# Routing steps on VectorE moved to other groups of an attention and mixture-of-experts kernel

## Chip, cores and metric

The kernel runs on one core of one Trainium2 chip, as one launch. The metric is the device time of that core in microseconds (us). Engines are named as the profile names them: PE is TensorE, with PEld its weight loads; DVE is VectorE, ACT is ScalarE, POOL is GpSimd and SP is SyncE, which issues most of the DMAs. Every engine works through its own instructions strictly in the order in which they stand, so an instruction that waits holds everything behind it on that engine.

## What is computed

Attention over 4 batches, 8 heads, 768 positions and 64 columns, in which a query sees only the keys of its own cluster, and behind it a mixture of 8 experts, where each of the 3072 tokens with a positive skip score goes to one expert:

```python
q_assign = np.argmax(np.einsum('bhsd,hcd->bhsc', q_n, c_n), axis=-1)   # k_assign likewise
scores = np.where(q_assign[:, :, :, None] == k_assign[:, :, None, :], scale * q @ k.T, -1e9)
attn = softmax(scores); x = (attn @ v)                  # 3072 tokens x 512
do_compute = x @ w_skip > 0
e_idx = np.argmax(x @ w_gate, axis=1); gate_w = softmax(x @ w_gate)[e_idx]
out = x + do_compute * gate_w * (relu(x @ w1[e_idx]) @ w2[e_idx])
```

## The kernel before

**Attention.** The work is cut into 16 pairs of heads, numbered 0 to 15; four pairs make a batch, so batch 0 is pairs 0 to 3. A pair has 24 slots. A slot computes one 128x384 block of scores with two matmuls (L637, L638), its exponential on ACT (L640, tile PT) and one accumulation of exponentials on POOL (L646, L652, tile acc). In the same slot PE also makes one matmul for the next pair (L588), whose row maximum DVE takes (L590, tile M). Behind slots 1, 9 and 17 of each pair PE has no scores for a while: it multiplies the last eight exponential tiles with the values (16 matmuls of L663), turns maxima (L612), and at one of the three places sums, turns and scales an earlier pair's output (L703, L715, L766 on PE; the reciprocal L720 and the scaling L771 on DVE). These three places of a pair are called block A (behind slot 1), block B (behind slot 9) and block C (behind slot 17) below. In a block DVE has no maxima to take, and the other DVE work of the kernel stands there.

**PSUM banks.** All of this takes its PSUM banks from one queue (`take`, `give`): a bank goes out again some three and a half slots after it was last taken. A matmul whose bank is still to be read waits for the reader. In block B the banks of L715 and L766 come round at slots 12 and 13, so PE waits there if L720 or L771 is late.

**Routing.** When a batch's four pairs are done, its 768 tokens are routed: the expert and the gate weight of each (`route_gates`), then its place in the expert's list (`route_slots`). The steps of `route_slots` that matter here, all on DVE but one:

- rk, rank, hi, los (L971 to L982): the token's rank in its expert, small operations;
- oht (L986, two instructions of 128x384 each): the one-hots of the rank; hs (L990), cs and cum (L1016, L1018), small;
- rhs (L1000, two instructions): the right sides of the list matmuls; then six small matmuls on PE (L1005) and their addition into slotacc (L1009);
- cc, c1, ri, li, gi, lo, code (L1026 to L1040): small.

**What sets the order.** Every step has a time in slots, counted from the start of a pair; a heap writes the instructions of all engines out in the order of these times, and that order is the program (nothing reorders it later). The 20 entries of a row of `SLOTS` are the times of the steps above, counted from the start of the batch's last pair. So 73.7, 81.7, 89.7 are blocks A, B, C of the third pair after the batch's last, 97.7 is block A of the fourth, and so on. The first row of `SLOTS` is for batches 0 and 1 (last pairs 3 and 7, so their steps lie in pairs 6 to 8 and 10 to 12), the second for batch 2 (last pair 11, so pairs 14 and 15). Batch 3 is routed in another way at the end. Also in pair 14, `early_lists` (`PLAN["early"]`) makes a first list of tokens out of batch 2's sums: a matmul (L1190), eight small operations on DVE and a gather by POOL (L1218).

**Experts.** Behind the attention the experts run one after the other, bound by PE; no line of that stage is touched.

Of the kernel before, what the change touches and what calls it, by code (L numbers as in the profile page):

```python
# [49 lines left out]
    "hi": (-38.405, -38.40), "masks": (-32.5, 0.12), "lo": (-30.38, -22.38), "copies": (-22.1, -21.2, -21.1),  # L50
    "smax": (-21.6, 1.0, -0.2), "mneg": (-9.2, 4.0), "mrows": ((-6.5, 0.2, 0.05), (9.62, 0.1, 0.05)),
    "av": 1.6, "oT": (0.35, 3.55), "sums": 33.55, "recip": 33.64, "xout": (33.66, 49.55, 41.55),
    "route": (33.45, 41.5, 65.5), "early": (85.4, 100.9),
}

GATES = (41.62, 41.63, 41.64, 41.65, 41.66, 49.66, 49.67, 49.68, 49.69, 49.7, 49.71, 50.5,
         53.16, 53.17, 53.18, 65.67, 65.68, 65.69, 65.7, 73.66, 73.67)
SLOTS = ((73.69, 73.7, 73.71, 73.72, 81.67, 81.68, 81.69, 81.7, 81.71, 81.72, 89.66, 91.0, 91.2,
          97.66, 97.67, 97.68, 97.69, 97.7, 97.71, 97.72),
         (73.69, 73.7, 73.71, 73.72, 73.73, 73.74, 73.75, 73.76, 73.77, 81.66, 81.67, 84.4, 84.6,  # L60
          85.9, 85.91, 97.66, 97.67, 97.68, 97.69, 97.7))
FIRST = {
    0: {
        "load_v": -18.9, "sims": -20.0, "hi": (-19.9, -19.8, -19.7, -19.6), "assign": (-19.0, 0.1, 0.01, 0.01, 0.01, 0.01),
# [20 lines left out]
class Kernel:  # L85
# [780 lines left out]
    def route_slots(self, i, bt):  # L866

        wait = iter([(t,) for t in SLOTS[i == self.npair - HP - 1]])
        yield from self.route_c(i, bt * KT, KT, wait)
# [316 lines left out]
    def early_lists(self, i):  # L1186

        nc, const = self.nc, self.const
        cp = self.take("cp", [P, 1])
        nc.tensor.matmul(cp, lhsT=self.ones_bf, rhs=self.cum[:, :1], start=True, stop=True)  # L1190
        yield (85.67,)
        pad = self.rt.tile([P, 1], F32, name="pad")
        nc.vector.tensor_scalar(out=pad, in0=cp, scalar1=-1.0, scalar2=float(P), op0=ALU.mult, op1=ALU.add)
        self.give("cp")
        nc.vector.tensor_scalar(out=pad, in0=pad, scalar1=0.0, scalar2=self.ident[:, :1], op0=ALU.max, op1=ALU.mult)
        nc.vector.tensor_tensor(out=self.cum[:, :1], in0=self.cum[:, :1], in1=pad, op=ALU.add)
        acc = self.acc[:, :, 0, :1]
        rd, wr = self.slot_ids(acc, const, P, 1, "e")
        self.xe = const.tile([P, 1, DM], F32, name="xe")
        yield 0.2  # L1200
        self.gather(self.xe[:, 0, :], rd, self.ntok - S)
        yield (91.66,)
        self.early = wr, self.slot_gates(acc, const, P, 1, "e")
# [329 lines left out]
```

## Time and profile before

| | us |
|---|---|
| time, median of 3 runs | 641.73 (641.08 to 643.89) |
| profiled execution, device time | 641.93 |
| profiled execution, span from first to last instruction | 640.2 |
| PE busy | 619.7 (97%) |
| DVE busy | 504.1 (79%) |
| ACT busy | 409.3 (64%) |
| POOL busy | 361.9 (57%) |

Attention takes roughly the first 430 us of the span. Times in rows are us from the span's start. A row of the view in order of time gives start, duration, engine, line, operation, output<-inputs with their shapes, how many instructions it merges, and in brackets the idle time of the engine before it with what ended that. A released wait is put down to the event that came last. A matmul's duration is that of a pipelined instruction: what a matmul costs is read from one start to the next.

### The profile page before, as it was taken

The page shows a single profiled execution, that of the slowest core. Times are in us where ns is not written, and L with a number is a line of the kernel's source. Part 1 is how long each engine was busy: PE and PEld are TensorE (multiplying, and loading weights), DVE is VectorE, ACT ScalarE, POOL GpSimd, SP SyncE. Part 2 cuts the span into 40 slices and gives each one's busy share as a digit, 9 for nine tenths or more (in the row PEclk, how much of TensorE's full clock was granted, in tenths as well). Part 3 has the DMA queues.
Part 4 walks back from the last instruction along what each step waited for, and adds up shares of the span by engine and source line. Part 5 has one row for each costly group of instructions (what it writes and reads, how often), then busy time and mean ns, then how long its engine had stood idle before and what let it go on. Part 6 is the DMA issues. An engine that isn't in the chain of part 4 may idle for free.

```text
span 640.2 us, 12142 instructions
## 1 busy us (share of the span) xinstructions
PE 619.7 (97%) x3873; PEld 459.1 (72%) x3873; DVE 504.1 (79%) x1060; ACT 409.3 (64%) x885; POOL 361.9 (57%) x384
## 2 busy tenths in 40 slices
PE   7899999999999999999999989999999999999994
PEld 3567677676766776767767756646799899899793
DVE  6989888789998789899879996875889765855721
ACT  7378677787777786777877867833744644645510
POOL 7797787777788777867867886522133212121101
PEclk9999999999999999999999999999999999999998
DMA  7388759758775665565565542332395766765711
GB/s 215 90 220 195 210 158 237 215 166 217 219 210 154 175 184 149 153 173 171 147 171 162 133 116 63 125 91 106 110 315 193 248 244 201 247 195 180 244 40 36
DMA packets 54321, 110.09 MB, mean 172 GB/s; under 512 B 8599, under 2 KB 22807, under 8 KB 54256
## 3 DMA queue, kind: packets, MB, share of 16 engines
q1 hardware_dynamic: 51232, 101.92, 54.9%
q0 software_dynamic: 2624, 7.18, 3.4%
q8 instruction: 32, 0.52, 0.4%
q14 instruction: 33, 0.27, 0.1%
q10 hardware_dynamic: 400, 0.20, 0.1%
HBM read 60.93 MB, written 10.55 MB: 112 GB/s over the span
## 4 chain that ended last, share of the span: by engine, by line
PE 31%; DMA 10%; issue 9%; DVE 4%; ACT 0%; POOL 0%; POOLq 0%; DVEq 0%
DMA out<-yo,idw 7%; PE ps L663 6%; PE ps L637 4%; PE ps L638 3%; PE ps L588 3%; DMA xg<-out,idr 2%; PE ph L1066 2%; PE ph L1065 2%; PE ph L1067 2%; PE py L1066 1%; PE py L1065 1%; PE py L1067 1%; DVE M L590 1%; DMA PT<-out,idr 1%; PE ps L703 1%
## 5 line engine op out<-in xcount | busy, mean ns | idle before, releaser
L652 POOL TENSOR_TENSOR acc<-acc,PT 128x384 f32<-128x384 f32 x246 | 242.2, 1013 | 47.3 <-ACT PT L640 46.9
L590 DVE TENSOR_REDUCE M<-ps 128x1 f32<-128x384 f32 x384 | 199.6, 554 | 24.8 <-PE ps L588 24.5
L640 ACT ACTIVATE PT<-ps 128x384 f32<-128x384 f32 x384 | 179.7, 492 | 41.2 <-PE ps L638 30.2
L637 PE MATMUL ps<-D 102*128 102x384 f32 x384 | 135.9, 354 | 3.9 <-DVE M L590 2.7
L663 PE MATMUL ps<-PT,vt 128*64 128x385 f32 x768 | 135.6, 494 | 0.0
L588 PE MATMUL ps<-D 96*128 96x384 f32 x384 | 130.3, 346 | 2.2 <-ACT D L568 1.0
L638 PE MATMUL ps<-D 128*128 128x384 f32 x384 | 130.2, 339 | 0.0
L663 PEld LDWEIGHTS ps<-PT,vt 128*64 128x64 f32 x768 | 50.8, 136 | 69.0 <-issue 59.3
L637 PEld LDWEIGHTS ps<-D 102*128 102x128 f32 x384 | 72.8, 190 | 24.5 <-issue 6.6
L646 POOL TENSOR_TENSOR acc<-PT 128x384 f32<-128x384 f32 x64 | 55.6, 888 | 52.0 <-ACT PT L640 51.2
L1223 POOL DMA_INDIRECT out<-yo,idw x15 | 20.1, 1337 | 112.9 <-DVE yo L1099 102.6
L588 PEld LDWEIGHTS ps<-D 96*128 96x128 f32 x384 | 73.1, 191 | 6.3 <-ACT D L568 1.4
L638 PEld LDWEIGHTS ps<-D 128*128 128x128 f32 x384 | 73.1, 190 | 0.0
L1351 ACT ACTIVATE hh<-ph 128x256 fp32r<-128x256 f32 x56 | 21.5, 384 | 46.4 <-PE ph L1067 46.1
L1352 DVE SCALAR_TENSOR_TENSOR hl<-ph,hh 128x256 fp32r<-128x256 f32 x56 | 23.7, 423 | 33.6 <-ACT hh L1351 33.5
L1323 ACT ACTIVATE D<-wraw 128x1024 fp32r<-128x1024 f32 (+1 forms) x45 | 44.1, 1002 | 6.2 <-PE py L1067 4.7
L1065 PE MATMUL ph<-x2l,D 128*128 128x256 f32 x168 | 47.7, 284 | 0.0
L1066 PE MATMUL ph<-x2h,D 128*128 128x256 f32 x168 | 47.5, 283 | 0.0
L1065 PE MATMUL py<-D,hh 128*128 128x512 f32 x112 | 45.0, 402 | 0.0
L623 ACT ACTIVATE D<-ps,blocks 6x256 fp32r<-6x256 f32 x84 | 33.3, 457 | 12.7 <-PE ps L612 12.3
L1324 DVE TENSOR_TENSOR D<-wraw,D 128x1024 fp32r<-128x1024 f32 (+1 forms) x29 | 34.3, 1184 | 6.2 <-ACT D L1323 5.3
L1066 PE MATMUL py<-D,hh 128*128 128x512 f32 x84 | 33.0, 392 | 0.0
(312 smaller groups left out, 1030.7 us busy)
## 6 DMA issues: line engine op xcount, KB each, us to landing
wraw<-w SPq DMA_DIRECT2D x72, 512.0 KB, 4.7
D<-D SPq DMA_DIRECT2D x124, 192.0 KB, 3.4
raw<-qk SPq DMA_DIRECT2D x16, 768.0 KB, 6.1
D<-raw SPq DMA_DIRECT2D x60, 192.0 KB, 3.6
vt<-v SPq DMA_DIRECT2D x16, 384.0 KB, 4.2
out<-x SPq DMA_DIRECT2D x31, 192.0 KB, 2.9
D<-mk SPq DMA_DIRECT2D x120, 24.0 KB, 2.3
out<-yo,idw POOLq DMA_INDIRECT x15, 4.6
```

The costliest lines, as they stand in the source:

```text
L588: nc.tensor.matmul(sm, lhsT=c["qm"][a][0:96, j * P:(j + 1) * P], rhs=c["kb"][a][0:96, hf * HALF:(hf + 1) * HALF], start=True, stop=True)
L590: nc.vector.tensor_reduce(out=c["m"][:, j, a, hf:hf + 1], in_=sm, axis=AX.X, op=ALU.max)
L637: nc.tensor.matmul(ps, lhsT=c["kb"][a][:MR, ks], rhs=c["qm"][a][:MR, sl], start=True, stop=False)
L638: nc.tensor.matmul(ps, lhsT=c["kc"][a][:, ks], rhs=c["qc"][a][:, sl], start=False, stop=True)
L640: nc.scalar.activation(out=pt, in_=ps, func=AF.Exp, scale=D ** -0.5)
L646: nc.gpsimd.tensor_tensor(out=acc, in0=self.pt(i, s - 2)[:, :HALF], in1=pt, op=ALU.add)
L652: (nc.vector if dve else nc.gpsimd).tensor_tensor(out=acc, in0=acc, in1=pt, op=ALU.add)
L663: nc.tensor.matmul(av[a * D:(a + 1) * D, :], lhsT=c["vt"][:, kt, a * D:(a + 1) * D], rhs=self.pt(i, hf * 2 * KT + kt * 2 + a), start=(kt = ...
L1065: mm(ps, lhsT=ah, rhs=bl, start=first, stop=False)
L1066: mm(ps, lhsT=ah, rhs=bh, start=False, stop=False)
L1323: nc.scalar.activation(out=h[:, cs], in_=r[:, cs], func=AF.Copy)
L1324: nc.vector.tensor_tensor(out=l[:, cs], in0=r[:, cs], in1=h.bitcast(F32)[:, cs], op=ALU.subtract)
```

## The change

Only times in the tables change, and with them the order. No instruction is added, removed or altered; the orders of ACT and SP stay the same, and on POOL the gather of `early_lists` stands one accumulation later.

```diff
-    "route": (33.45, 41.5, 65.5), "early": (85.4, 100.9),
+    "route": (33.45, 41.5, 65.5), "early": (86.1, 100.9),
...
-SLOTS = ((73.69, 73.7, 73.71, 73.72, 81.67, 81.68, 81.69, 81.7, 81.71, 81.72, 89.66, 91.0, 91.2,
+SLOTS = ((73.69, 73.7, 73.71, 73.72, 81.67, 89.66, 89.67, 89.68, 89.69, 105.66, 105.67, 107.3, 107.5,
...
         cp = self.take("cp", [P, 1])
         nc.tensor.matmul(cp, lhsT=self.ones_bf, rhs=self.cum[:, :1], start=True, stop=True)
-        yield (85.67,)
+        yield (86.3,)
```

For batches 0 and 1 the second one-hot, hs, cs and cum go from block B to block C of pairs 6 and 10; both right sides go to block B of pairs 7 and 11 (they stood in blocks B and C of pairs 6 and 10), with their matmuls and the addition behind them; cc to li go from block A to block C of pairs 7 and 11, gi to code to block A of pairs 8 and 12. For batch 2 both one-hots, hs, cs and cum go from block A to block B of pair 14, ahead of the right sides, which stay there; its matmuls, the addition, cc, c1 and the steps of `early_lists` come 0.6 to 0.7 slots later.

DVE in pair 6 (batch 0), from block B on, before; rows is the last step of the next pair's cluster assignment, M the maxima, raw a subtraction for a later pair:

```order
L534 STREAM_TRANSPOSE rows<-oh 128x384
L986 TENSOR_TENSOR oht<-iota,los 128x384 x2
L990 TENSOR_TENSOR hs<-iota,hi 128x12
L1016 TENSOR_REDUCE cs<-ohd 128x8
L1018 TENSOR_TENSOR cum<-cum,cs 128x8
L1000 TENSOR_TENSOR rhs_2091<-rv,hs 128x30x8
L720 RECIPROCAL rs<-ps_87 128x3x2 x2
L771 TENSOR_TENSOR x<-ps_85,rs 128x384
```

The same place now:

```order
L534 STREAM_TRANSPOSE rows<-oh 128x384
L986 TENSOR_TENSOR oht<-iota,los 128x384
L720 RECIPROCAL rs<-ps_87 128x3x2 x2
L771 TENSOR_TENSOR x<-ps_85,rs 128x384
L590 TENSOR_REDUCE M_200<-ps_81 128x1
```

Only one one-hot is left between the assignment and the reciprocal; the other, hs, cs and cum stand in block C behind raw, where the second right side stood.

DVE in pair 14 (batch 2), block A to block B, as a piece of the difference:

```order
 L982 SCALAR_TENSOR_TENSOR los<-hi,rank 128x6
+L590 TENSOR_REDUCE M_200<-ps_84 128x1
+L590 TENSOR_REDUCE M_200<-ps_83 128x1
+L604 TENSOR_REDUCE MX_190<-M_199 128x3x2
+L590 TENSOR_REDUCE M_200<-ps_87 128x1
+L590 TENSOR_REDUCE M_200<-ps_85 128x1
+L590 TENSOR_REDUCE M_200<-ps_86 128x1
+L590 TENSOR_REDUCE M_200<-ps_88 128x1
+L590 TENSOR_REDUCE M_200<-ps_82 128x1
+L590 TENSOR_REDUCE M_200<-ps_85 128x1
 L986 TENSOR_TENSOR oht<-iota,los 128x384 x2
 L990 TENSOR_TENSOR hs<-iota,hi 128x12
```

The eight maxima of slots 2 to 9 now come ahead of the one-hots, and the one-hots stand where only the two right sides stood ahead of L720.

DVE in pair 7, block B, now (before, L534 was followed by L720 at once):

```order
L534 STREAM_TRANSPOSE rows<-oh 128x384
L1000 TENSOR_TENSOR rhs_2346<-rv,hs 128x30x8 x2
L720 RECIPROCAL rs<-ps_87 128x3x2 x2
L771 TENSOR_TENSOR x<-ps_85,rs 128x384
L590 TENSOR_REDUCE M_199<-ps_86 128x1
L590 TENSOR_REDUCE M_199<-ps_88 128x1
L1009 TENSOR_TENSOR slotacc<-slotacc,ps_84 128x80
```

Both right sides now stand ahead of the reciprocal of that block, and the addition into slotacc behind two maxima; pair 11 has the same.

## Rows read from the trace of the kernel before

**Rows 1.** In order of time, DVE, pair 6, block B.

```profile
181.38 1.87 DVE L986 TENSOR_TENSOR oht<-iota,los 128x384 bf16<-128x384 f32 x2
183.18 0.16 DVE L990 TENSOR_TENSOR hs<-iota,hi 128x12 bf16<-128x12 f32 x1
...
183.60 0.40 DVE L1000 TENSOR_TENSOR rhs<-rv,hs 128x240 bf16<-128x240 bf16 x1
183.92 0.26 DVE L720 RECIPROCAL rs<-ps 128x6 f32<-128x6 f32 x2
```

**Rows 2.** In order of time, DVE, pair 7, block B.

```profile
206.58 0.58 DVE L534 STREAM_TRANSPOSE rows<-oh 128x384 bf16<-128x384 bf16 x1
207.98 0.27 DVE L720 RECIPROCAL rs<-ps 128x6 f32<-128x6 f32 x2 [0.82 <-PE ps L715]
```

**Rows 3.** In order of time, PE, pair 6: L637 of slots 10 and 15.

```profile
182.31 0.42 PE L637 MATMUL ps<-D 102*128 102x384 f32 x1
...
186.09 0.34 PE L637 MATMUL ps<-D 102*128 102x384 f32 x1
```

**Rows 4.** The same two slots of pair 7.

```profile
208.02 0.42 PE L637 MATMUL ps<-D 102*128 102x384 f32 x1
...
210.72 0.34 PE L637 MATMUL ps<-D 102*128 102x384 f32 x1
```

**Rows 5.** Busy time by stretch: PE, PEld, DVE, ACT, POOL, granted clock, DMA share, GB/s.

```profile
381.50:385.00 3.50, 3.50 (x16) 1.24 (x16) 3.49 (x6) 1.88 (x4) 3.35 (x4) 0.51 0.00 0
...
183.00:186.00 3.00, 2.49 (x13) 1.92 (x12) 2.83 (x11) 1.87 (x5) 1.89 (x2) 1.00 0.59 146
```

**Rows 6.** In order of time, DVE, pair 14, block A.

```profile
375.83 1.70 DVE L986 TENSOR_TENSOR oht<-iota,los 128x384 bf16<-128x384 f32 x2
377.45 0.82 DVE L990 TENSOR_TENSOR hs<-iota,hi 128x12 bf16<-128x12 f32 x1
...
379.14 1.01 DVE L590 TENSOR_REDUCE M<-ps 128x1 f32<-128x384 f32 x2
```

**Rows 7.** In order of time, PE, pair 14: L637 of slots 5, 6, 9 and 10.

```profile
376.38 0.34 PE L637 MATMUL ps<-D 102*128 102x384 f32 x1
...
379.74 0.44 PE L637 MATMUL ps<-D 102*128 102x384 f32 x1 [2.67 <-DVE M L590]
...
381.45 0.43 PE L637 MATMUL ps<-D 102*128 102x384 f32 x1
...
387.88 0.42 PE L637 MATMUL ps<-D 102*128 102x384 f32 x1
```

**Rows 8.** In order of time, PE, pair 13: L637 of slots 9 and 10.

```profile
354.81 0.34 PE L637 MATMUL ps<-D 102*128 102x384 f32 x1
...
359.69 0.42 PE L637 MATMUL ps<-D 102*128 102x384 f32 x1
```

**Rows 9.** In order of time, DVE, pair 13, block B.

```profile
356.37 0.57 DVE L516 TENSOR_TENSOR eqc<-eqc,wts 128x384 f32<-128x384 f32 x1
...
359.64 0.27 DVE L720 RECIPROCAL rs<-ps 128x6 f32<-128x6 f32 x2 [0.81 <-PE ps L715]
```

**Rows 10.** In order of time, DVE, pair 14, block B.

```profile
383.03 2.08 DVE L1000 TENSOR_TENSOR rhs<-rv,hs 128x240 bf16<-128x240 bf16 x2
387.83 0.27 DVE L720 RECIPROCAL rs<-ps 128x6 f32<-128x6 f32 x2 [2.72 <-PE ps L715]
```

**Rows 11.** In order of time, POOL, pair 13, through block B.

```profile
353.86 6.04 POOL L652 TENSOR_TENSOR acc<-acc,PT 128x384 f32<-128x384 f32 x6
```

**Rows 12.** In order of time, POOL, pair 7, up to the end of block B.

```profile
204.80 3.42 POOL L652 TENSOR_TENSOR acc<-acc,PT 128x384 f32<-128x384 f32 x3
```

**Rows 13.** In order of time, PE, pair 6: list matmuls in slot 19, and what follows.

```profile
191.62 0.39 PE L1005 MATMUL ps<-rhs,oht 128*128 128x80 bf16 x6
191.84 0.42 PE L588 MATMUL ps<-D 96*128 96x384 f32 x1
```

**Rows 14.** In order of time, DVE, pair 6, behind block C's right side.

```profile
191.47 0.56 DVE L590 TENSOR_REDUCE M<-ps 128x1 f32<-128x384 f32 x1 [0.21 <-PE ps L588]
```

More of the change, by code (lines that the diff above doesn't have):

```diff
@@ L57 @@
          53.16, 53.17, 53.18, 65.67, 65.68, 65.69, 65.7, 73.66, 73.67)
-SLOTS = ((73.69, 73.7, 73.71, 73.72, 81.67, 81.68, 81.69, 81.7, 81.71, 81.72, 89.66, 91.0, 91.2,
-          97.66, 97.67, 97.68, 97.69, 97.7, 97.71, 97.72),
-         (73.69, 73.7, 73.71, 73.72, 73.73, 73.74, 73.75, 73.76, 73.77, 81.66, 81.67, 84.4, 84.6,
-          85.9, 85.91, 97.66, 97.67, 97.68, 97.69, 97.7))
+SLOTS = ((73.69, 73.7, 73.71, 73.72, 81.67, 89.66, 89.67, 89.68, 89.69, 105.66, 105.67, 107.3, 107.5,
+          113.66, 113.67, 113.68, 113.69, 121.66, 121.67, 121.68),
+         (73.69, 73.7, 73.71, 73.72, 81.66, 81.67, 81.68, 81.69, 81.7, 81.71, 81.72, 85.0, 85.2,
+          86.6, 86.61, 97.66, 97.67, 97.68, 97.69, 97.7))
 FIRST = {
```

## Prediction

> **What bounds the kernel now.** The first view to read is the page's busy times: PE is busy 97% of the span, so time can only be won where PE stands still or runs slowly. The second is the view in order of time for PE, read from the start of one score matmul (L637) to the next: an undisturbed slot takes 0.54 us, as slots 10 to 15 of pair 7 show (210.72 - 208.02 = 2.70 for five) [rows 4]. Measured in this way two kinds of place stand out among the slots that the change touches.
>
> The first is pair 6 behind block B. The same five slots take 186.09 - 182.31 = 3.78 us there [rows 3], 1.08 more than in pair 7, which has no routing step in that block. The view in order of time for DVE says why: the one-hots, hs, cs, cum and a right side stand ahead of the reciprocal L720, which begins 1.61 us behind slot 10's L637 (183.92 against 182.31) [rows 1, 3], while in pair 7 it begins 0.04 us ahead of it [rows 2, 4]. So it was 1.65 us late and cost PE 1.08: the first 0.57 us of lateness cost nothing, because the banks come round only later. Pair 10 repeats this (there are two such places).
>
> The second is pair 14. From slot 5 to slot 6 PE takes 379.74 - 376.38 = 3.36 us, 2.82 too many, and the wait is for a maximum on DVE [rows 7]. DVE came late because both one-hots, hs, cs and cum stood ahead of the maxima, from 375.83 to 379.14 [rows 6]. Behind that wait comes a second loss: from slot 9 to slot 10 PE takes 387.88 - 381.45 = 6.43 us [rows 7], in pair 13 only 359.69 - 354.81 = 4.88 [rows 8]. In this stretch the granted clock is 0.51, which is about the lower of the two levels, 1.2 GHz [rows 5]. PE had been idle for 2.67 us shortly before. DVE isn't the cause of this second loss: it had finished the right sides and waited 2.72 us for PE [rows 10]. I put these 1.55 us to the clock, and so to the wait.
>
> **Pairs 6 and 10.** One one-hot stays in block B, and hs, cs, cum, the second one-hot and the right side leave it. Two one-hots took 183.18 - 181.38 = 1.80 us [rows 1], so one takes about 0.9 or less. In pair 7 DVE was idle for 0.82 us ahead of L720 [rows 2], and with the 0.57 that cost nothing there are 1.39 us for it. The wait goes: 1.08 us twice, 2.16. In block C a one-hot (0.9) and the small steps (183.60 - 183.18 = 0.42) [rows 1] replace a right side (between 0.32 and the 1.04 of pair 14 [rows 10]); behind it DVE waited 0.21 for PE [rows 14]. The new work of 1.32 is 0.3 to 1.0 longer, so it ends 0.1 to 0.8 behind the point at which PE is ready, about the 0.57 that cost nothing. I cost it at nothing, and 0.2 at most.
>
> **Pairs 7 and 11.** Two right sides come in ahead of L720. Each took 0.32 us with nothing beside it (183.60 to 183.92) [rows 1], and 1.04 in pair 14 [rows 10]: 0.64 to 2.08 together. They have the 0.82 of idle time and the 0.57, 1.39 us. So the cost lies between nothing and 0.69. I take it from POOL's row: its additions go on until 208.22 [rows 12], 1.06 us after DVE is free (206.58 + 0.58 = 207.16) [rows 2]. The second right side probably waits for that, and the first holds POOL up by 0.3, so 1.06 + 0.3 + 0.32, about 1.7: it costs 0.3 each, 0.6 for both pairs. The six list matmuls come along; they cost PE 191.84 - 191.62 = 0.22 us [rows 13] in slot 19 of pair 6 now and in slot 11 of pair 7 then: no difference. Queued behind the right sides are the reciprocal, the scaling and the maxima, and PE's slots 12 and 13 wait for these, which is what the 0.3 counts. The small steps from cc to code leave a block A and go into a block C and a later block A, where DVE has idle time; nothing there, with at most 0.2 for a block C.
>
> **Pair 14, block A.** With the one-hots gone, DVE begins the first maximum at 375.83 instead of 379.14 [rows 6], 3.31 us earlier. The wait was 2.82, so it goes whole with 0.49 to spare. The stretch at the lower clock goes with it: 2.82 + 1.55 = 4.37 us.
>
> **Pair 14, block B.** Here the moved work meets the right sides, and all of it stands ahead of L720. Pair 13 has the same block without a stall: DVE is free for its first step there at 356.37, and L720 begins at 359.64 [rows 9], 3.27 us later; with 0.57 the room is 3.84. In the trace of before there were 2.72 us to spare [rows 10], but 1.55 of them came from PE's slow stretch, which goes. The cost of the chain from both sides: 1.80 + 0.42 + 0.64 = 2.86 with the durations of pair 6 [rows 1], and 3.31 + 2.08 = 5.39 with those of pair 14 [rows 6, 10]. So PE loses between nothing and 1.55 us.
>
> What decides is POOL. The operation hs took 0.16 us in pair 6 and 0.82 in pair 14, block A [rows 1, 6]: it waits for an addition of POOL to end. The Trainium skill has the rule for this: in "SBUF — State Buffer", section "Who interferes with whom", a DVE instruction with two SBUF inputs and a GpSimd instruction that reads SBUF share one port pair, and the one that issued first keeps it for its whole length. By that rule alone, with an addition always running, every one-hot, hs, cum and right side would wait, and block B would come out at the upper bound (it is the second rival). Pair 13's row says how long additions run: six in 6.04 us, until 359.90 [rows 11], 3.53 after DVE is free. I let the one-hots, hs and cum wait for them, add 0.3 by which DVE holds POOL up, and let the right sides run free: 3.5 + 0.3 + 0.64, about 4.4 us. That is 0.56 over the room, and so is the loss. The later matmuls, the addition into slotacc, and the steps of `early_lists` stand 0.6 slots later and ahead of the same av matmuls; DVE has caught up there or catches up in block C, and POOL's gather, queued one addition later, delays only additions whose sum is asked for a block later. I cost this at nothing, and 0.3 at most.
>
> **The sum.** 2.16 - 0.6 + 4.37 - 0.56 = 5.4 us. The profiled execution took 641.93 us, 0.20 over the median, and would come to 636.5; from the median it is 641.73 - 5.4 = 636.3 us. Behind pair 14 the chain of waits goes on through PE and DVE, and the weights are asked for as buffers come free, so I expect what is won there to be kept.
>
> **The rivals.** First, the gain of pair 14 is given back later, because something in pair 15 or at the start of the experts comes at a fixed time, a weight load for instance. Then pairs 6, 7, 10 and 11 remain: 2.16 - 0.6 = 1.6, so 640.2 us. Against it: those loads are issued when split steps free their buffers, and these move along. Second, the stall only moves into block B of pair 14. Every step meets an addition, the chain takes 5.39, PE waits 1.55 there, and the lower clock follows once more with its 1.55; pairs 7 and 11 lose 0.69 each. That is 2.16 - 1.38 + 4.37 - 3.10 = 2.05, so 639.7 us. For it: DVE in block A showed just these durations [rows 6]. Against it: POOL runs out of work before the right sides [rows 11]. Third, on the slower side: the lower clock follows short waits as well. Then pairs 7 and 11 lose 0.69 + 1.55 each and pair 14 loses 3.10: 7.58 lost against 6.53 won, so 642.8 us. It decides from the point at which a wait of 0.7 us is enough to bring the lower clock. Against it: pair 6 lost 1.08 at one place, and the granted clock there stayed 1.00 [rows 5].
>
> **How the numbers follow.** The forecast with its bounds has 0.77: from 635.2 (all costs nothing, 6.53 won) to 638.1 (all costs at their upper end, 3.6 won), most likely 636.3. The first rival has 0.08, the second 0.12, the third 0.03. The range goes from 634.6, which is the best case less the 0.65 by which the fastest run lies under the median, to 639.4, which takes in most of the second rival. A measurement of this kernel can tell about 0.5% from no change, 3.2 us: faster means under 638.5. That is the forecast's case and a little of the second rival's, 0.78; the same 0.20; slower 0.02.
>
> **What would show it.** In the changed trace, slot 5 to slot 6 of pair 14 should take 0.54 us, slot 9 to slot 10 between 4.8 and 5.0 with the clock at 1.00, and slots 10 to 15 of pair 14 some half microsecond more than undisturbed ones. Slots 10 to 15 of pair 6 should take 2.7 us, and those of pair 7 about 3.2, 0.22 of it for the list matmuls. The forecast is wrong if PE waits for L720 or L771 by over 1.5 us in pair 14, or over 0.7 in pair 7, or if pair 15 grows.

## The result, and the profile after

The changed kernel takes 636.85 us (median of 5 runs, 636.57 to 637.49) where the kernel before takes 641.73: a ratio of 0.992, with a 95% interval from 0.990 to 0.994. The forecast was 636.3, in a range from 634.6 to 639.4. The profiled execution took 636.83 us with a span of 635.1, so the median needs no correction. The page's row of busy times:

```profile
PE 616.7 (97%) x3873; PEld 460.3 (72%) x3873; DVE 508.7 (80%) x1060; ACT 409.1 (64%) x885; POOL 361.7 (57%) x384
```

PE is busy 3.0 us less with the same 3873 matmuls, and the span is 5.1 shorter. So the gain has both parts that the prediction named: matmuls that ran at the lower clock, and waits. The interval lies clear of 1, so the gain of 0.8% is clear of the noise.

A pair's length, read from slot 0's L637 to the next pair's, is the unit of what follows (pair 15 has no next pair; its length is read to the L637 of its own slot 23). The pairs that the change doesn't touch keep their length to 0.01 us in before and after (24.35, 26.35 and 24.62 recur), with one exception: pair 2, where PE waits for a transfer of inputs, takes between 24.91 and 25.96 in the executions of this study, in no order that follows the edits. In before's profile it took 25.07 and in after's 25.85, so 0.78 us of the difference between these two profiles is that transfer. What the change did to the other pairs, in us; the forecast column is the prediction's terms, with its 0.22 for each batch's list matmuls taken out of pairs 6 and 10 and put into 7 and 11:

| | before | after | difference | forecast |
|---|---|---|---|---|
| pairs 6 and 10 | 25.73, 25.69 | 24.35, 24.35 | -2.72 | -2.60 |
| pairs 7 and 11 | 24.33, 24.33 | 24.71, 24.71 | +0.76 | +1.04 |
| pair 14 | 29.24 | 24.93 | -4.31 | -3.81 |
| start of pair 15 to the end | 240.46 | 241.06 | +0.60 | 0 |
| sum | | | -5.67 | -5.37 |

The growth of the last row lies in pair 15: its length is 26.60 us before and 27.25 after, 0.65 more, and what follows it is equal within 0.05.

**Pairs 6 and 7.** PE in order of time, L637 alone, first pair 6 (slots 10 and 15), then pair 7 (slots 10, 11, 12 and 15):

```profile
182.94 0.42 PE L637 MATMUL ps<-D 102*128 102x384 f32 x1
...
185.64 0.34 PE L637 MATMUL ps<-D 102*128 102x384 f32 x1
...
207.28 0.42 PE L637 MATMUL ps<-D 102*128 102x384 f32 x1
207.90 0.34 PE L637 MATMUL ps<-D 102*128 102x384 f32 x1
208.73 0.34 PE L637 MATMUL ps<-D 102*128 102x384 f32 x1
...
210.33 0.34 PE L637 MATMUL ps<-D 102*128 102x384 f32 x1
```

Pair 6 takes 185.64 - 182.94 = 2.70 us for five slots, where it took 3.78 [rows 3]. Pair 7 takes 3.05 where it took 2.70 [rows 4]; slot 11, the one with the list matmuls, is 208.73 - 207.90 = 0.83 long, 0.31 more than its neighbours. DVE in block B of pair 7 says why so little is lost beyond that:

```profile
206.34 1.58 DVE L1000 TENSOR_TENSOR rhs<-rv,hs 128x240 bf16<-128x240 bf16 x2
207.84 0.25 DVE L720 RECIPROCAL rs<-ps 128x6 f32<-128x6 f32 x2
```

The two right sides take 1.58 us together; the second begins at 206.86 and has 1.06 of them, as expected. L720 begins 207.84 - 207.28 = 0.56 us behind slot 10's L637: the point up to which lateness was free in pair 6 of before was 0.57.

**Pair 14.** PE (slots 5, 6, 9, 10, 12 and 15), DVE through block B, and the granted clock (columns as in [rows 5]):

```profile
375.06 0.34 PE L637 MATMUL ps<-D 102*128 102x384 f32 x1
375.59 0.34 PE L637 MATMUL ps<-D 102*128 102x384 f32 x1
...
377.18 0.34 PE L637 MATMUL ps<-D 102*128 102x384 f32 x1
382.06 0.42 PE L637 MATMUL ps<-D 102*128 102x384 f32 x1
...
383.21 0.34 PE L637 MATMUL ps<-D 102*128 102x384 f32 x1
...
385.44 0.34 PE L637 MATMUL ps<-D 102*128 102x384 f32 x1
```

```profile
378.38 2.21 DVE L986 TENSOR_TENSOR oht<-iota,los 128x384 bf16<-128x384 f32 x2
380.51 0.97 DVE L990 TENSOR_TENSOR hs<-iota,hi 128x12 bf16<-128x12 f32 x1
...
381.66 0.63 DVE L1018 TENSOR_TENSOR cum<-cum,cs 128x8 bf16<-128x8 bf16 x1
382.22 0.71 DVE L1000 TENSOR_TENSOR rhs<-rv,hs 128x240 bf16<-128x240 bf16 x2
382.85 0.25 DVE L720 RECIPROCAL rs<-ps 128x6 f32<-128x6 f32 x2
```

```profile
380.00:384.00 4.00, 4.00 (x27) 2.78 (x24) 3.85 (x10) 3.43 (x8) 2.73 (x4) 1.00 0.00 0
```

Slot 5 to 6 takes 0.53 us (3.36 before) and slot 9 to 10 takes 4.88 (6.43 before) [rows 7]; the clock is 1.00 through the stretch. The chain ahead of L720 took 382.85 - 378.38 = 4.47 us. POOL's additions beside it ended at 376.23 + 6.03 = 382.26, just as the right sides began:

```profile
376.23 6.03 POOL L652 TENSOR_TENSOR acc<-acc,PT 128x384 f32<-128x384 f32 x6
```

Slots 12, 13 and 14 took 0.63, 0.94 and 0.66, together 2.23, where before had 0.75, 0.74 and 0.54, together 2.03, its list matmuls included: block B costs PE 0.2.

**Pair 15.** Here stands what the forecast didn't have. PE from slot 5's L637 to slot 6's, DVE and POOL of after:

```profile
399.82 0.42 PE L637 MATMUL ps<-D 102*128 102x384 f32 x1
...
403.42 0.55 PE L612 MATMUL ps<-ident,MX 128*128 128x128 f32 x3 [0.93 <-DVE MX L604]
403.72 0.42 PE L637 MATMUL ps<-D 102*128 102x384 f32 x1
```

```profile
395.81 3.45 DVE L1032 CAST ri<-rank 128x6 int32<-128x6 f32 x1
...
401.23 2.04 DVE L1061 TENSOR_TENSOR rawW<-wraw,D 128x1024 fp32r<-128x1024 f32 x1
403.20 0.16 DVE L604 TENSOR_REDUCE MX<-M 128x6 f32<-128x18 f32 x1
```

```profile
392.06 7.16 POOL L652 TENSOR_TENSOR acc<-acc,PT 128x384 f32<-128x384 f32 x8
399.52 1.69 POOL L646 TENSOR_TENSOR acc<-PT 128x384 f32<-128x384 f32 x2 [0.30 <-ACT PT L640]
```

Slot 5 to 6 takes 403.72 - 399.82 = 3.90 us, and 408.36 - 405.46 = 2.90 in before. PE waits for the maximum MX, which DVE is late with: the cast ri, six numbers in each partition, took 3.45 us ahead of it. It ends at 399.26, and POOL's run of additions ends at 392.06 + 7.16 = 399.22. In before the same cast took 0.44, also inside a run of additions (DVE and POOL of before):

```profile
401.45 0.44 DVE L1032 CAST ri<-rank 128x6 int32<-128x6 f32 x1
```

```profile
398.25 5.40 POOL L652 TENSOR_TENSOR acc<-acc,PT 128x384 f32<-128x384 f32 x6 [0.18 <-ACT PT L640]
```

At slot 14 the pair is 0.35 us shorter than before (2.94 before, 2.59 after). That isn't the 1.0 coming back: slot 14 takes 2.58 to 2.61 in every kernel below with the later list steps, with a long ri or a short one, and 2.93 or 2.94 in every one with the old times. So the later list steps win 0.35 there, and the pair as a whole loses 0.65.

### The profile page after: what moved, and what is told of

It is laid out like the page before. It is cut to its first block, busy times and chain, and to the rows that moved or that the text cites. A ratio compares the mean times of both kernels' runs of the same rounds, so it can differ in the third digit from the quotient of the medians.

```text
span 635.1 us, 12144 instructions
## 1 busy us (share of the span) xinstructions
PE 616.7 (97%) x3873; PEld 460.3 (72%) x3873; DVE 508.7 (80%) x1060; ACT 409.1 (64%) x885; POOL 361.7 (57%) x384
## 4 chain that ended last, share of the span: by engine, by line
PE 80%; DMA 8%; issue 7%; DVE 3%; ACT 1%; POOL 1%; SPq 0%; POOLq 0%; DVEq 0%; ACTq 0%
PE ps L663 20%; PE ps L637 11%; PE ps L588 10%; PE ps L638 10%; DMA out<-yo,idw 3%; PE ph L1067 3%; PE ph L1066 3%; PE ph L1065 3%; DMA raw<-qk 3%; PE py L1066 2%; PE py L1065 2%; PE py L1067 2%; PE ps L766 2%; PE ps L494 2%; PE ps L703 2%
## 5 line engine op out<-in xcount | busy, mean ns | idle before, releaser
L637 PE MATMUL ps<-D 102*128 102x384 f32 x384 | 136.1, 354 | 0.8 <-DMA raw<-qk 0.6
L637 PEld LDWEIGHTS ps<-D 102*128 102x128 f32 x384 | 73.2, 191 | 20.6 <-issue 6.6
L646 POOL TENSOR_TENSOR acc<-PT 128x384 f32<-128x384 f32 x64 | 54.0, 862 | 49.9 <-ACT PT L640 49.0
```

The costliest lines, as they stand in the source:

```text
L637: nc.tensor.matmul(ps, lhsT=c["kb"][a][:MR, ks], rhs=c["qm"][a][:MR, sl], start=True, stop=False)
L646: nc.gpsimd.tensor_tensor(out=acc, in0=self.pt(i, s - 2)[:, :HALF], in1=pt, op=ALU.add)
```

## The experiments

Ratios are to the kernel before, run again on the same chip: its median was 641.79 us beside the first four kernels, 643.05 beside those with the one-hots back and the old list times, and 642.63 beside the one with both remedies. The intervals are about 0.4% wide (some 2.4 us), so differences of 1 us between these kernels are read from the lengths of pairs and not from the times. A kernel with one time alone was run once.

**The changed kernel once more.** No edit.

> The changed kernel itself, beside the others on the same chip. Theory: 636.9 us, ratio to the kernel before 0.992. In its first trace pair 15's slot 5 to 6 took 3.90 us against 2.90 before, with the cast ri on DVE taking 3.45 us in block A. If that is a property of the order, it shows here again (3.3 to 3.6 us); if it was chance of one execution, ri takes under 1.1 us and the time between slots 5 and 6 is 2.9.

637.18 us, ratio 0.993 (0.991 to 0.995). ri took 3.46 us and slot 5 to 6 of pair 15 took 3.89. So the long cast is no accident of one execution.

**Batches 0 and 1 alone.** The second row of `SLOTS` and the times of `early_lists` as before:

```diff
-    "route": (33.45, 41.5, 65.5), "early": (86.1, 100.9),
+    "route": (33.45, 41.5, 65.5), "early": (85.4, 100.9),
...
-         (73.69, 73.7, 73.71, 73.72, 81.66, 81.67, 81.68, 81.69, 81.7, 81.71, 81.72, 85.0, 85.2,
-          86.6, 86.61, 97.66, 97.67, 97.68, 97.69, 97.7))
+         (73.69, 73.7, 73.71, 73.72, 73.73, 73.74, 73.75, 73.76, 73.77, 81.66, 81.67, 84.4, 84.6,
+          85.9, 85.91, 97.66, 97.67, 97.68, 97.69, 97.7))
...
-        yield (86.3,)
+        yield (85.67,)
```

> Only batches 0 and 1 routed in the new order, batch 2 as before. Theory of the prediction (three independent places): pairs 6 and 10 fall from 25.7 to 24.35 us, pairs 7 and 11 grow by 0.38 to 24.71, pair 14 stays at 29.2 with its wait of 2.7 us and its stretch at half clock; 2.0 us saved, 639.8 us. Rival (the places are coupled: POOL or the banks carry a delay on): pair 14's length changes by over 0.5 us, and the saving is under 1 or over 3 us.

640.74 us, ratio 0.997 (0.996 to 0.999); 639.8 was expected. Pairs 6, 7, 10 and 11 took 24.35, 24.71, 24.35 and 24.71, the same as in the full change (the 2.0 us that were expected), and pair 14 took 29.20. Its wait of 2.68 us was there, and so was the lower clock, but at another point of it. PE (L637 of slots 6, 9 and 10) and the clock of that stretch:

```profile
379.37 0.69 PE L637 MATMUL ps<-D 102*128 102x384 f32 x1 [2.68 <-DVE M L590]
...
382.41 0.48 PE L637 MATMUL ps<-D 102*128 102x384 f32 x1
387.45 0.42 PE L637 MATMUL ps<-D 102*128 102x384 f32 x1
```

```profile
379.40:382.40 3.00, 3.00 (x9) 3.00 (x10) 2.45 (x6) 0.99 (x3) 1.44 (x3) 0.50 0.00 0
```

In before, three slots behind the wait ran at full pace (379.74 to 381.45 [rows 7]) and then the clock fell. Here it was 0.50 at once. Slots 6 to 8 cost 382.41 - 379.37 = 3.04 instead of 1.59, and slot 9 took 5.04 instead of 4.88: 1.61 us in all, where before lost 1.55. In these two traces the drop begins at different points and takes nearly the same.

**Batch 2 alone.** The first row of `SLOTS` as before:

```diff
-SLOTS = ((73.69, 73.7, 73.71, 73.72, 81.67, 89.66, 89.67, 89.68, 89.69, 105.66, 105.67, 107.3, 107.5,
-          113.66, 113.67, 113.68, 113.69, 121.66, 121.67, 121.68),
+SLOTS = ((73.69, 73.7, 73.71, 73.72, 81.67, 81.68, 81.69, 81.7, 81.71, 81.72, 89.66, 91.0, 91.2,
+          97.66, 97.67, 97.68, 97.69, 97.7, 97.71, 97.72),
```

> Only batch 2 routed in the new order, batches 0 and 1 as before. Theory: pair 14 falls from 29.2 to 24.9 us (wait 2.8 and half clock 1.55 gone, 0.2 to 0.6 paid in block B), pair 15's slot 5 to 6 pays 1.0 for the cast ri; 3.3 to 3.7 us saved, 638.2 us, and with the kernel of batches 0 and 1 alone the savings add up to the 4.9 of the whole change. Rival (pair 15 pays because the earlier pairs moved): slot 5 to 6 of pair 15 is 2.9 us and the saving 4.3 us.

638.57 us, ratio 0.995 (0.993 to 0.997). Pair 14 took 24.96 us, and ri 3.46, so the loss of pair 15 belongs to batch 2's part. By the ratios the two halves save 1.7 and 3.3 us, together 4.9, and the whole 4.7, with some 1.1 us of uncertainty on each; the pairs, which took the same in the halves as in the whole within 0.05 us, show that they add up.

**The five small steps earlier.** ri to code move from block A of pair 15 to stand behind c1 in pair 14:

```diff
-          86.6, 86.61, 97.66, 97.67, 97.68, 97.69, 97.7))
+          86.6, 86.61, 86.62, 86.63, 86.64, 86.65, 86.66))
```

> The changed kernel with ri, li, gi, lo and code of batch 2 directly behind c1 in pair 14 instead of in block A of pair 15. Theory (the cast ri waits for POOL's run of additions and makes the maxima's turn and L771 late): those five steps take under 1 us in all, where POOL waits for the gather anyway, slot 5 to 6 of pair 15 falls from 3.90 to 2.9 us, and the time is 1.0 us below the changed kernel, 635.9. Rival (pair 15 is late because POOL and DVE are behind anyway, the cast is only what is seen waiting): another DVE step waits there, slot 5 to 6 stays at 3.6 to 3.9, and the time stays at 636.9.

635.75 us, ratio 0.991 (0.989 to 0.993): 1.4 us under the changed kernel by the medians, 0.8 by the ratios. DVE:

```profile
386.52 0.16 DVE L1032 CAST ri<-rank 128x6 int32<-128x6 f32 x1
...
387.00 0.16 DVE L1040 TENSOR_TENSOR code<-c,gi 128x6 f32<-128x6 f32 x1
```

All five end 0.64 us after the first began. Pair 15's slot 5 to 6 is back at 2.90 us, the pair takes 26.24 instead of 27.25, and pair 14 is as long as before the move (24.94). So the five steps in their old place, of which the cast is the long one, cost the 1.0 us. This version has the shortest pairs of all that compute the whole result; against the kernel before it is clearly faster, and against the changed kernel by this 1.0 us, which the pair lengths show better than the medians do.

**The one-hots back in block A.** The rest of the change stays:

```diff
-         (73.69, 73.7, 73.71, 73.72, 81.66, 81.67, 81.68, 81.69, 81.7, 81.71, 81.72, 85.0, 85.2,
+         (73.69, 73.7, 73.71, 73.72, 73.73, 73.74, 81.68, 81.69, 81.7, 81.71, 81.72, 85.0, 85.2,
```

> The changed kernel with both one-hots of batch 2 back in block A of pair 14; hs, cs and cum stay in block B. DVE then begins the first maximum there 1.6 to 2.0 us later than in the changed kernel; 0.5 of that is spare, so PE should wait 1.1 to 1.5 us from slot 5 to 6. Theory (the half clock follows a wait only when it is long): the wait alone is paid, slots 6 to 10 run at the granted clock 1.00 with 4.88 us from slot 9 to 10, block B of pair 14 loses nothing, and the time is 0.9 to 1.3 us over the changed kernel. Rival (any wait of this kind brings it): some 1.5 us more are lost in slots 6 to 10 at a granted clock near 0.5, and the time is 2.4 to 2.8 us over.

638.03 us, ratio 0.993 (0.991 to 0.995). PE (L637 of slots 6, 9 and 10) and the clock behind the wait:

```profile
376.33 0.44 PE L637 MATMUL ps<-D 102*128 102x384 f32 x1 [0.98 <-DVE M L590]
...
378.04 0.34 PE L637 MATMUL ps<-D 102*128 102x384 f32 x1
382.92 0.42 PE L637 MATMUL ps<-D 102*128 102x384 f32 x1
```

```profile
378.50:382.50 4.00, 4.00 (x29) 1.54 (x28) 3.94 (x8) 2.98 (x5) 3.39 (x4) 1.00 0.02 4
```

Slot 5 to 6 takes 1.67 us, 1.14 too many, and nothing follows: slot 9 to 10 is 4.88 and the clock 1.00. Pair 14 is 1.02 longer than in the changed kernel. So this wait of 0.98 us cost only itself, where the one of 2.67 cost half as much again. That fits the prediction, which put the 1.55 us of before to the long wait; it is one trace of each kernel, and the section on the forecast has two traces of one kernel that differ.

**POOL's additions left out** around block B of pair 14 and behind it, so that the sums lack those exponentials:

```diff
+        if i == self.npair - 2 and s in (6, 7, 8, 9, 18, 19, 20, 21, 22, 23):
+            return
         if kt == 1:
```

> The changed kernel without POOL's accumulations of slots 6 to 9 and 18 to 23 of pair 14 (those exponentials are missing in the sums; all else is computed). Theory (DVE's operations in block B and the cast ri in pair 15 wait for these additions): the chain from the first one-hot to the reciprocal L720 falls from 4.47 us to 2.6 to 3.0, slots 12 to 14 of pair 14 take 0.2 us less, ri takes under 0.3 us instead of 3.45, and slot 5 to 6 of pair 15 takes 2.9 us. Rival (the operations are slow by themselves or through DMA): chain and ri stay within 0.4 us of what they were.

634.93 us. DVE, the same chain as above (two lines stand ahead of it, so L988 is L986 and L722 is L720):

```profile
377.61 1.02 DVE L988 TENSOR_TENSOR oht<-iota,los 128x384 bf16<-128x384 f32 x2
378.54 0.16 DVE L992 TENSOR_TENSOR hs<-iota,hi 128x12 bf16<-128x12 f32 x1
...
378.98 0.72 DVE L1002 TENSOR_TENSOR rhs<-rv,hs 128x240 bf16<-128x240 bf16 x2
381.24 0.27 DVE L722 RECIPROCAL rs<-ps 128x6 f32<-128x6 f32 x2 [1.55 <-PE ps L717]
```

The one-hots take 1.02 us instead of 2.21, hs 0.16 instead of 0.97, the right sides 0.72 as before. The chain ends 2.1 us after it began instead of 4.47, so 2.4 us of it were spent on POOL. PE got only 0.19 of that back (pair 14 took 24.74): the block has room for the rest. The rule that the prediction drew on, from "SBUF — State Buffer" of the Trainium skill, section "Who interferes with whom" (a DVE instruction with two SBUF inputs and a GpSimd instruction that reads SBUF hold each other off), agrees with this pair of traces. ri took 0.16 us here, with the additions of slots 18 to 23 gone as well: the long cast needs them.

**The list steps at their old times,** with the one-hots in block B as in the change:

```diff
-    "route": (33.45, 41.5, 65.5), "early": (86.1, 100.9),
+    "route": (33.45, 41.5, 65.5), "early": (85.4, 100.9),
...
-         (73.69, 73.7, 73.71, 73.72, 81.66, 81.67, 81.68, 81.69, 81.7, 81.71, 81.72, 85.0, 85.2,
-          86.6, 86.61, 97.66, 97.67, 97.68, 97.69, 97.7))
+         (73.69, 73.7, 73.71, 73.72, 81.66, 81.67, 81.68, 81.69, 81.7, 81.71, 81.72, 84.4, 84.6,
+          85.9, 85.91, 97.66, 97.67, 97.68, 97.69, 97.7))
...
-        yield (86.3,)
+        yield (85.67,)
```

> The changed kernel with the later steps of batch 2 (list matmuls, addition, cc, c1, the steps of the early list) at their old times, so only the one-hots, hs, cs and cum are moved in pair 14. Theory (POOL's run of additions reaches into block A of pair 15 with or without 0.6 slots in the gather): ri still takes 2.5 us or more, slot 5 to 6 of pair 15 stays at 3.5 to 3.9, and the time is within 0.5 us of the changed kernel. Rival (the gather's delay is what makes POOL late there): ri takes under 1.1 us, slot 5 to 6 takes 2.9 and 1.0 us is won.

636.89 us, ratio 0.991 (0.989 to 0.993). The theory missed and the rival held. DVE and POOL:

```profile
395.64 0.45 DVE L1032 CAST ri<-rank 128x6 int32<-128x6 f32 x1
```

```profile
390.60 7.25 POOL L652 TENSOR_TENSOR acc<-acc,PT 128x384 f32<-128x384 f32 x8
```

The run of eight additions is there, until 397.85, and ri begins inside it, but takes 0.45 us; slot 5 to 6 of pair 15 is 2.90 and pair 14 is 24.91. So one part of the change, the list steps and the gather 0.6 to 0.7 slots later, brings the long cast. This part wins nothing in pair 14; what it wins is the 0.35 at slot 14 of pair 15, which took 2.93 here.

**A product and a cast in ri's old place.** As with the five steps earlier, plus two small operations that nobody uses:

```diff
-          86.6, 86.61, 97.66, 97.67, 97.68, 97.69, 97.7))
+          86.6, 86.61, 86.62, 86.63, 86.64, 86.65, 86.66, 97.66, 97.67))
...
+        if i == self.npair - HP - 1:
+            yield next(wait)
+            p0 = self.rt.tile([P, KT], F32, name="probe0")
+            vec.tensor_tensor(out=p0, in0=rank, in1=c1, op=ALU.mult)
+            yield next(wait)
+            p1 = self.rt.tile([P, KT], I32, name="probe1")
+            vec.tensor_copy(p1, rank)
```

> The kernel with ri to code moved behind c1, and in block A of pair 15, where ri stood, two small DVE operations whose results nothing reads: first a product of two SBUF tiles of 128x6, later a copy of 128x6 to integers as ri is. Theory (an operation with two SBUF inputs gets in at the end of the running addition, a copy that also needs the shared write side waits until POOL has nothing queued): the product takes 0.2 to 1.1 us, the copy lasts until POOL's run ends, 1.5 us or more. Rival (whoever comes there waits for the whole run): the product takes over 2 us. Second rival (the wait of ri was a matter of where in an addition it arrived): both take under 1.1 us.

634.91 us; the product took 0.15 us and the cast 0.44. So neither a two-input operation nor a cast of this size waits for long at that place merely by standing there; the theory missed, and the times are those of the second rival, which the next experiments test.

**Casts at other times of an addition.** The five steps earlier, and 18 unused casts of six numbers in pairs 1 to 5, 8, 9, 12 and 13, beside POOL's additions:

```diff
+        if i in (1, 2, 3, 4, 5, 8, 9, 12, 13):
+            for t in ((4.5, 6.5) if i % 2 else (5.5, 7.5)):
+                add(t, self.probe)
...
+    def probe(self, i):
+        t = self.rt.tile([P, KT], I32, name="probe")
+        self.nc.vector.tensor_copy(t, self.iota[:, :KT])
```

> The kernel with ri to code behind c1, and in addition a copy of 128x6 to integers that nothing reads, twice in each of pairs 1, 2, 3, 4, 5, 8, 9, 12 and 13, between maxima of slots 4 to 7 while POOL adds without a pause. Theory (it depends on where in an addition the copy arrives): copies that arrive in the first quarter of an addition wait through several of them (over 1.5 us), copies that arrive in its middle or later get in at its end (under 0.7 us); both kinds occur. Rival (ri was held by something that is there only in block A of pair 15): every one of the 18 copies takes under 1.1 us.

636.68 us. The row of the line gives the shortest, the median and the longest, in ns:

```profile
L388 DVE CAST probe<-iota x18: 156/606/1004, 51.2 to 355.2; 128x6 int32<-128x6 f32 x18
```

A cast that arrived 0.03 to 0.09 us into an addition took 0.80 to 1.00, one that arrived 0.28 to 0.33 in took 0.56 to 0.61, one that arrived 0.41 to 0.47 in took 0.42 to 0.48: each waited for the running addition to end, and for no more. The theory, that some points of arrival make a cast wait through several additions, missed.

**Both remedies,** the five steps earlier and the list steps at their old times:

```diff
-    "route": (33.45, 41.5, 65.5), "early": (86.1, 100.9),
+    "route": (33.45, 41.5, 65.5), "early": (85.4, 100.9),
...
-         (73.69, 73.7, 73.71, 73.72, 81.66, 81.67, 81.68, 81.69, 81.7, 81.71, 81.72, 85.0, 85.2,
-          86.6, 86.61, 97.66, 97.67, 97.68, 97.69, 97.7))
+         (73.69, 73.7, 73.71, 73.72, 81.66, 81.67, 81.68, 81.69, 81.7, 81.71, 81.72, 84.4, 84.6,
+          85.9, 85.91, 85.92, 85.93, 85.94, 85.95, 85.96))
...
-        yield (86.3,)
+        yield (85.67,)
```

> The changed kernel with ri to code behind c1 and the later steps of batch 2 at their old times: both ways out of pair 15's loss at once. Theory (they mend the same loss): pair 15's slot 5 to 6 takes 2.9 us, pair 14 24.9, and the time is that of the kernel with ri early alone, 0.991 of the kernel before and 1.0 us under the changed kernel. Rival (the gather's earlier place has a worth of its own): another 0.5 us or more in pairs 14 and 15.

635.71 us, ratio 0.989 (0.988 to 0.991). Pair 14 took 25.23 us, where 24.9 was expected, and pair 15 26.59: together 0.64 more than with the five steps earlier alone (24.94 and 26.24). The two remedies mend the same loss, and the second one gives up the 0.35 of slot 14. In pair 14 a subtraction was held up. DVE and POOL:

```profile
389.83 2.63 DVE L1061 TENSOR_TENSOR rawW<-wraw,D 128x1024 fp32r<-128x1024 f32 x1
```

```profile
389.56 1.82 POOL L652 TENSOR_TENSOR acc<-acc,PT 128x384 f32<-128x384 f32 x2
```

L1061 takes 1.22 us where nothing holds it up, so it waited 1.4 us, longer than either of the two additions: until the run ended at 391.38. So ri isn't the only instruction that lost to a run.

**Other points of arrival for ri itself,** with one small reduction ahead of it, and ten casts behind one to three such reductions in other pairs:

```diff
+        for t, n in {2: ((7.5, 1),), 4: ((5.5, 2), (7.5, 1)), 8: ((5.5, 1), (7.5, 2)), 12: ((5.5, 3), (7.5, 3)),
+                     5: ((4.5, 1),), 9: ((4.5, 2),), 13: ((6.5, 1),)}.get(i, ()):
+            add(t, self.probe, n)
...
+        if i == self.npair - HP - 1:
+            self.small_steps(1)
         vec.tensor_copy(ri, rank)
```

> The changed kernel (ri in block A of pair 15 again) with one small reduction of 18 columns, which reads SBUF through one input only, ahead of ri, so that ri arrives some 0.08 us later in POOL's addition; and nine copies to integers in earlier pairs, each behind one to three such reductions, at other points of an addition. Theory (ri lost because of the very point at which it arrived): ri now takes under 1.0 us, slot 5 to 6 of pair 15 takes 2.9 to 3.1 instead of 3.9, and among the nine copies one that arrives near 0.17 into an addition may take over 1.5 us. Rival (something particular to that place holds it, whatever the point): ri still takes over 3 us, and the nine copies all take under 1.1 us.

636.37 us. DVE, ri's place (moved to L1047 by the lines added):

```profile
396.22 3.38 DVE L1047 CAST ri<-rank 128x6 int32<-128x6 f32 x1
```

ri arrived 0.26 us into an addition instead of 0.17 and still took 3.38 us; the ten others took 0.24 to 0.93 and ended with the running addition. So it isn't the point of arrival alone.

**The subtraction away from the gather.** In all five executions so far with a long ri (after, once more, batch 2 alone, one-hots back, other points of arrival) the gather took 1.66 to 1.96 us, and in all eight others 1.22; in those five, a subtraction of a weight piece (L1061) had begun 0.35 to 0.65 us ahead of the gather. Here it comes one maximum later in the changed kernel:

```diff
-        for w, k, part, t in ((0, 0, 0, -14.35), (0, 1, 0, -14.34), (0, 0, 1, -6.3), (0, 2, 0, -6.2), (0, 3, 0, 1.68),
+        for w, k, part, t in ((0, 0, 0, -14.35), (0, 1, 0, -14.34), (0, 0, 1, -5.5), (0, 2, 0, -6.2), (0, 3, 0, 1.68),
```

> The changed kernel with one step moved: the 128x1024 subtraction of a weight piece (L1061, 1.22 us, two SBUF inputs) stands one maximum later on VectorE in pair 14, which puts it behind slot 18's scores, so that it begins only after GpSimd's gather (L1218) and not 0.4 us ahead of it. Nothing else changes. Theory: the gather that begins while this subtraction runs (1.94 us long, 1.22 in the kernels without the loss) is what leads to the 3.4 us cast in pair 15. Then the gather takes 1.22 us, the cast ri at most 1.0, slot 5 to slot 6 of pair 15 takes 2.9 us instead of 3.9, and pair 14 is up to 0.6 us longer because maxima come 1.2 us later. Rival: the two only go together by the order of the program. Then the gather takes 1.22 but ri still over 3 us and slot 5 to 6 about 3.9 us. If the gather stays at 1.7 or more with no subtraction beside it, the subtraction isn't what lengthens it.

636.78 us. DVE and POOL:

```profile
394.94 6.52 DVE L1032 CAST ri<-rank 128x6 int32<-128x6 f32 x1
```

```profile
388.46 1.22 POOL L1218 DMA_INDIRECT xe<-out,idre  x1 [2.54 <-DVE M L590]
...
390.55 8.29 POOL L652 TENSOR_TENSOR acc<-acc,PT 128x384 f32<-128x384 f32 x8
...
400.44 0.98 POOL L652 TENSOR_TENSOR acc<-acc,PT 128x384 f32<-128x384 f32 x1
```

The gather took 1.22 us, so it was the subtraction that lengthened it. But ri didn't get shorter: it took 6.52 us, until 401.46, and POOL's run, now without a pause, ended at 401.42. Slot 5 to 6 of pair 15 took 4.92 us and the pair 28.27. The theory missed for the loss; what held is that gather and long cast only went together. It also shows the wait most plainly: 6.48 us of the run were left when ri began, where 3.41 were left in after, and ri took nearly twice as long. (The time is no worse than the changed kernel's because pair 2 took 24.91 us in this execution and 25.85 in after's.)

## Why the forecast came out right, step by step

**Pairs 6 and 10: as worked out.** 1.08 was forecast for each behind block B, and slots 10 to 15 gave 3.78 - 2.70 = 1.08. The whole pairs gained 1.38 and 1.34; the rest is the list matmuls that left. Block C, costed at nothing, shows no loss.

**Pairs 7 and 11: right mechanism, smaller size.** The term was 0.3 each beside list matmuls of 0.22. Measured is 0.38 in all, of which slot 11, with the list matmuls, has 0.31; 0.07 is left for the wait. The list matmuls cost more than their 0.22 when read from slot to slot, but they do so in pairs 6 and 10 as well and cancel. The right sides took 1.58 us, not 1.7, and ended at the edge of what is free.

**Pair 14, block A: right in size, the clock's part with some luck.** 2.82 of wait and 1.55 of lower clock were forecast to go, and 3.36 - 0.53 = 2.83 and 6.43 - 4.88 = 1.55 went. The waits of 2.67 and 2.68 us were followed by the lower clock in both traces that have them; the 0.98 with the one-hots put back was not, and neither was one of 1.65 us that PE had in pair 15 with the subtraction moved (its clock behind it):

```profile
401.97 1.49 PE L833 MATMUL ps<-oT,wg 128*32 128x384 f32 x12 [1.65 <-DVE x L771]
```

```profile
401.90:406.00 4.10, 3.95 (x29) 2.38 (x31) 3.97 (x13) 2.82 (x7) 0.35 (x1) 1.00 0.52 167
```

But the length of a wait alone doesn't decide. At the start of the attention PE waits 1.41 us, until 19.57 in after and until 19.71 in the second trace of the same kernel. The first was followed by the lower clock, the second was not (their rows in this order):

```profile
22.00:24.00 2.00, 2.00 (x7) 2.00 (x7) 1.93 (x5) 1.11 (x3) 0.47 (x1) 0.50 0.04 8
```

```profile
22.00:24.00 2.00, 1.61 (x10) 1.29 (x8) 1.93 (x4) 1.13 (x3) 0.84 (x1) 1.00 0.04 8
```

So the 1.55 us of before may not be there every time either. Of the 39 executions of before beside the experiments, five had a mean granted clock of 0.997 and took 639.97 to 640.49 us; the others had 0.987 to 0.994 and took 641.33 to 643.93. A stretch like that of pair 14 takes about 0.003 off the mean (an estimate: 0.49 of 3.5 us in 640). So those five probably ran without it; no trace of one was kept, and this is not shown.

**Pair 14, block B: chain right, loss too high.** The chain was put at 4.4 us and took 4.47; the loss was put at 0.56 and came out at 0.2. What failed is the room of 3.84 us, which is pair 13's. There DVE came to the block 356.37 - 354.81 = 1.56 us behind slot 9's L637 [rows 8, 9]; in pair 14 it came 378.38 - 377.18 = 1.20 behind it, so the room was 0.36 larger. The 0.57 of pair 6 held: L720 began 382.85 - 382.06 = 0.79 us behind slot 10's L637, 0.22 past what is free, and cost 0.2. The second rival, every step held up and the lower clock again, didn't come: the right sides ran free (0.71 for two), because POOL had run out of work at 382.26, as the row of pair 13 said it would.

**Pair 15: the step that failed.** The prediction let the list steps and the gather come later, said that the gather "delays only additions whose sum is asked for a block later", and costed this at nothing, or 0.3 at most. Slot 5 to 6 of that pair lost 1.0 us, the pair 0.65 in all, and with the list steps at their old times the 1.0 was gone. "If pair 15 grows" was one of the prediction's own signs of being wrong, and pair 15 grew: on this point it was wrong, though its time came out. It is the first rival's direction, gain given back in pair 15, by a mechanism that none of the rivals named, and with 1.0 us instead of 3.81: the cast ri waited through a run of additions. hs at 0.82 instead of 0.16 [rows 6] had shown that small DVE steps wait on POOL, and the prediction used this for block B but not for the small steps of pair 15, whose place in the order hadn't changed. A wait through several additions stood in no row of before, where ri took 0.44, so its size couldn't be foreseen from them.

**The third rival** (lower clock after short waits in pairs 7, 11 and 14) didn't come: PE had no such waits there, and the one of 0.98 us with the one-hots put back brought no lower clock.

**The sum.** Term by term the forecast's 5.4 us stands against 5.67 measured in the pairs: 0.40 more won in pairs 6 to 11, 0.50 more in pair 14, 0.60 lost from pair 15 on. The errors cancel in part, and that the total is within 0.3 us of the forecast is luck to that extent. One of the prediction's bounds is added up wrongly: 3.6 us won is all 6.53 less 1.38 and 1.55, and leaves out the 0.2, 0.2 and 0.3 that it had allowed for the two places in block C and for the later steps; with them it is 2.9 won, 638.8 us instead of 638.1. Its range, up to 639.4, takes that in. The medians differ by 4.9, and the profiled executions by 5.1 with 0.78 lost to pair 2's transfer, which the change doesn't touch.

**What stays open** is why ri waits for the whole run. Shown: it needs POOL's additions (0.16 without them); it comes with the list steps and the gather later (0.45 without that); it ends with the run (3.45 and 6.52 us in runs of different length). Not enough for it by themselves: the gather's own length, the point of arrival, a cast as such. One rival is untested, and the traces speak for it in part: how far POOL is behind. Counted from the end of an exponential on ACT to the start of its addition, the addition that ran when ri began was 1.88 to 2.28 us late in all six long cases. It was 1.25 to 1.27 late where ri took 0.44 to 0.46 in pair 15, 1.78 beside the unused cast there, and at most 1.04 beside the 28 unused casts, so these never met a POOL as late as that. It can't be lateness alone: a one-hot in pair 6 of before began beside an addition 2.36 us late and waited for that one only. The page of the Trainium skill named above says that of a cast in its two-port form and GpSimd the one that issues first has the port for one instruction's length; the 28 unused casts agree (none over 1.00 us), ri doesn't, six times out of six where the later list steps, ri's old place and POOL's additions met.

## What to carry to other kernels

Before moving an instruction, look at who reads SBUF on GpSimd at the place where it goes and also at the places whose order it leaves alone but whose neighbours it shifts: a small VectorE step there can cost a whole run of additions. Small steps that nobody waits for soon are best put where GpSimd is idle; these five cost 0.64 us there and 5.3 in pair 15 (3.45 + 0.78 + 0.16 + 0.79 + 0.15). And a wait on TensorE should be priced with what may follow it: the one of 2.67 us cost 4.4, the one of 0.98 cost 1.1, and whether the lower clock follows can differ between executions of one kernel.

## What the runs showed of the hardware that was not expected

- A cast of 128x6 from f32 to int32 took 0.16 us alone, 0.16 to 1.00 in 28 places beside additions of GpSimd, and 3.38 to 6.52 at one place, where it ended within 0.05 us of the end of the run of additions. A subtraction of 128x1024 with two SBUF inputs, 1.22 us where nothing held it up, did the same once and took 2.63.
- After an idle time of 2.67 us the granted clock of TensorE fell to 0.51 only 1.7 us after work had begun again (379.74 to 381.45 at full pace), and after one of 2.68 in another order at once, at 0.50; both cost some 1.6 us. After 0.98 and 1.65 us of idling in the same stage it stayed at 1.00; after 1.41 at the start of the attention it fell to 0.50 in one execution and stayed at 1.00 in another of the same kernel.
- A gather by GpSimd that began 0.37 us into a VectorE subtraction with two SBUF inputs took 1.94 us, ending 1.09 after the subtraction, and 1.22 with that subtraction moved away.
